# A long-convolution filter turned by VectorE in 32x32 blocks instead of by TensorE, and loaded in sixteen pieces

## The chip, the cores and the metric

The kernel runs on one core of one Trainium2 chip. The metric is device time in microseconds (us) of one execution, the median of several runs. A core has a matrix engine (TensorE, PE in the profile, with its weight loads as PEld), a vector engine (VectorE, DVE), a scalar engine (ScalarE, ACT), a general engine (GpSimd, POOL), a queue engine that here issues most transfers (SyncE, SP), and 16 DMA engines that carry out the transfers of all queues. Each engine works through its own list in order and waits on semaphores for the others.

## What is computed

The reference joins a long convolution with a gated feed-forward network. Cut to what matters:

```python
xn = _layernorm(A_q)                                   # 2048 x 512
k_shift = sum over t of k_pad[:, t:t+S, :] * shift_k   # four taps
kv = k_shift * v
y  = irfft(rfft(kv, 2S) * rfft(ssm_k, 2S))[:S] + kv * ssm_D
s  = xn * y
h  = gelu(xn @ w_gate) * (xn @ w_up)                   # 512 -> 1792
g  = silu(h @ w_down)                                  # 1792 -> 512
return A_q + s * g
```

The filter of the long convolution, `ssm_k`, is 512 channels by 2048 positions in bf16, 2 MB.

## The kernel before, in words

The tokens are cut into four quarters of 512. For each quarter, layer norm makes `XN`, a transpose makes `xnT`, 14 units of 128 hidden columns make the gate and up products (4 matmuls of 512 columns each), GELU and product fill `HT`, and the down products follow. The weights of gate and up come in four column parts (`FC`, line 793): part 0 serves units 0 and 1, part 1 units 2 to 5, part 2 ("third weights") units 6 to 9, part 3 units 10 to 13.

The convolution is a two-stage Fourier transform by matmuls. Stage 1 of the filter (`stage1("H", u)`, lines 956 to 991) multiplies the table `F1` with slice `u` of the turned filter `HTr`, for u from 0 to 7, in two products `i` of 512 columns, of two matmuls each; product `i` needs the row blocks 2i and 2i+1. The results go by ScalarE or VectorE to SBUF and then to a DRAM buffer `ZH`. The shift of k by four taps runs on VectorE (`kshift`, lines 1003 to 1029, 32 instructions of 2048 elements) and is multiplied with v; stage 1 of that product and stage 2 of both follow.

`ssm_k` lies in DRAM with channels as rows, and stage 1 needs positions on partitions. `load_h(k)` (line 820) loads 128 channels, rows of 4 KB, into `Hn[:, k, :]`. `h_transpose(k)` (lines 923 to 939) reads `Hn` as 32-bit words, two bf16 each, and turns it by eight TensorE transposes of 128x128 words (line 931, with an FP32 identity that line 696 makes on GpSimd), four into each of two PSUM banks; two instructions of VectorE or ScalarE (lines 638 and 641) bring them to `HTr`. Position 16a + 2t + (0 or 1) ends at partition a, slice t. `h_fold` (line 945, GpSimd) adds `ssm_D` to position 0 once all four row blocks are there; only the two products of slice 0 need it.

The order of work is written out. `ORDER` (line 26) is the order of the loads; all of them are issued by SP, and `SEQ` (line 27) lists all other tasks by number, from which each engine's list follows; a "b" marks the second choice of engine. `LAND` holds the planner's assumed landing times; they only serve its choice of buffers. Loads come first in SP's list, then the transposes by DMA, the ZK stores and so on. In TensorE's list before, the turning stands between the units: row blocks 0 and 1 after the gate product of unit 5, the rest up to the first products of units 6 to 9. GpSimd's list has the four copies of taps (line 1001) and the fold in between. The function `bass.AP` takes a list of [step, count], outermost first.

Of the kernel before, what the change touches and what calls it, by code (L numbers as in the profile page):

```python
# [16 lines left out]
NT = 16  # L17
# [8 lines left out]
ORDER = "x00 x01 x02 w0 w1 D0 h0 h1 h2 h3 s0 k0 w2 x1 k1 k2 w3 d0 d1 v0 v1 k3 v2 v3 x2 x3"  # L26
SEQ = (
# [25 lines left out]
LAND = {"x0_0": 2900, "h0": 11200, "x0_1": 3400, "x0_2": 4900, "D": 9850, "wg0": 5850, "wu0": 6800, "h1": 12500, "wg1": 8300, "wu1": 9800, "h2": 13850, "h3": 15500, "sk": 18000, "kh1": 19200, "kh113": 19400, "kz": 10800, "k0": 20600, "wg2": 22100, "wu2": 23600, "x1": 24900, "k1": 26200, "k2": 27500, "wg3": 29650, "wu3": 31200, "wd0": 33450, "wd1": 35700, "v0": 37050, "v1": 38400, "k3": 39750, "v2": 41100, "v3": 42450}  # L53
# [365 lines left out]
def build_kernel(nc, A_q, A_k, A_v, A_shift_k, A_ssm_k, A_ssm_D, B_w_gate, B_w_up, B_w_down, out):  # L419
    with ExitStack() as es0:  # L420
# [11 lines left out]
        def new(name, shape, dt):  # L432
            h = at(name, shape, dt, place["at"])
            place["at"] += size(shape, dt)
            return h
# [15 lines left out]
        ident32 = new("ident32", [128, 128], FP32)  # L451
# [91 lines left out]
        R_id, R_id32 = res("ident", ident[:]), res("ident32", ident32[:])  # L543
# [21 lines left out]
        R_Hn = [res(f"Hn{k}", Hn[:, k, :]) for k in range(KD)]  # L565
        R_HTr = [[res(f"HTr{t}_{k}", HTr[:, t, 256 * k:256 * k + 256]) for k in range(KD)] for t in range(NT // 2)]
# [96 lines left out]
        bHTr = [[B(f"HTr{k}_{h}") for h in range(2)] for k in range(KD)]  # L663
# [31 lines left out]
        def pool_id32():  # L695
            P(lambda h: h.tensor_scalar(ident32[:], K32[:], 0.0, None, ALU.is_equal), [R_id32], [R_K32])

# [15 lines left out]
        bcq, bck, bid32 = B("cq"), B("ck"), B("id32")  # L713
# [5 lines left out]
        S.add([("POOL", 560.0)], lambda e: pool_id32(), r=[bk32], w=[bid32])  # L719
# [72 lines left out]
        h_dr = A_ssm_k.rearrange("(kd p) n -> p kd n", p=128)  # L792
# [27 lines left out]
        def load_h(k, ring):  # L820
            load(f"h{k}", Hn[:, k, :], h_dr[:, k, :], [R_Hn[k]], [bHn[k]], 524288, ring)
# [99 lines left out]
        t_htr = [[] for _ in range(KD)]  # L921

        def h_transpose(k):
            pp = [B(f"psh{k}_{h}", pX) for h in range(2)]

            def tr(hf):
                def f(e):
                    for j in range(4):
                        o = bank(pp[hf])[:, 128 * j:128 * (j + 1)]
                        src = Hn[:, k, :].bitcast(FP32).rearrange("p (a t) -> p t a", t=NT // 2)[:, 4 * hf + j, :]  # L930
                        trk.op("PE", lambda h, o=o, src=src: h.transpose(o, src, ident32[:]), r=[R_Hn[k], R_id32], w=R_bank(pp[hf]), accum=True)  # L931
                return f
            for hf in range(2):
                h_tr_tasks.append(S.add([("PE", 4 * 110.0)], tr(hf), r=[bid32, bHn[k]], w=[pp[hf]], lat=150.0))
            for hf in range(2):
                def ev(e, h, hf=hf):
                    return copy(e, h, HTr[:, 4 * hf:4 * hf + 4, 256 * k:256 * (k + 1)], bank16(pp[hf]).rearrange("p (t x) -> p t x", x=256))
                t_htr[k].append(op([("ACT", act(1024)), ("DVE", dve(1024, 2))], ev, r=[pp[hf]], w=[bHTr[k][hf]],
                   rr=lambda hf=hf: R_bank(pp[hf]), ww=[x[k] for x in R_HTr[4 * hf:4 * hf + 4]]))

        for k in range(KD):
# [4 lines left out]
                    r=[bHD, *[bHTr[k][0] for k in range(KD)]], w=[bFold], rr=[R_D, *R_HTr[0]], ww=R_HTr[0])  # L946
# [9 lines left out]
        def stage1(x, u, Z):  # L956
# [11 lines left out]
            if x == "H":  # L968
                bl = B(f"low{u}")
                for i in range(2):  # L970
                    def pairs(e, i=i):
                        for b in range(2):
                            k = slice(64 * b, 64 * b + 64)
                            trk.op("PE", lambda h, b=b, k=k: h.matmul(ps(psl(pp[i]), b), lhsT=F1[k, :], rhs=HTr[k, u, 512 * i:512 * i + 512], start=True, stop=True, tile_position=(64 * b, 0)),  # L974
                                   r=[R_F1, *R_HTr[u][2 * i:2 * i + 2]], w=[R_ps[psl(pp[i])][b]], accum=True)
                    s1_tasks[x].append(S.add([("PE", T_FWD)], pairs, r=[bF1] + [bHTr[k][u // 4] for k in range(2 * i, 2 * i + 2)] + ([bFold] if u == 0 else []), w=[pp[i]], lat=150.0, mode=2))
# [403 lines left out]
```

## Time and profile before

| what | value |
|---|---|
| median of 3 runs | 188.6 us (188.5 to 189.69) |
| profiled execution | 188.14 us |
| its span, first to last instruction | 186.3 us |
| granted TensorE clock | 1.0 throughout |
| `Hn` loads in the profile | 4 of 512 KB, median 7.7 us from issue to landing |
| bytes read from HBM, written | 27.39 MB, 14.68 MB |

The page gives, for each engine, its busy time and share of the span; then a chain of work that ended last, followed back from the last instruction; then groups of instructions by line, with the number, the busy time in us, the mean of one in ns, and the idle time ahead of them with what ended it. In rows of the timeline and of the chain in order of time, the first number is the start in us, the second the length in us. In the view by stretches, "(x60)" is the number of instructions and "DMA share" the busy share of the 16 DMA engines.

### The profile page before, as it was taken

The numbers are of one execution on the slowest core, as the hardware profiler recorded it, in microseconds if no ns is written. First come the engines' busy times: TensorE is split into PE (matmuls) and PEld (weight loads), VectorE is DVE, ScalarE is ACT, GpSimd is POOL, SyncE is SP. The second block draws the span as 40 slices with busy tenths as digits, with TensorE's granted clock in tenths as the row PEclk, the third lists the DMA queues.
The fourth block names the chain that finished last, engine by engine and source line by source line (L and its number), as shares of the span: only waits on it lengthen the run. The fifth ranks groups of instructions, "written<-read, shape, count | busy, mean of one in ns | idle before, by whom it ended". The sixth has DMA issues, their size and how long they took to land.

```text
span 186.3 us, 3672 instructions
## 1 busy us (share of the span) xinstructions
PE 181.4 (97%) x1448; PEld 79.8 (43%) x1456; DVE 165.9 (89%) x250; ACT 137.9 (74%) x193; POOL 12.8 (7%) x27
## 2 busy tenths in 40 slices
PE   8899999999999999999999999999999999999993
PEld 2675544434343343344344334334343434445552
DVE  7868999999999999997499989999999987347995
ACT  4675897998589989995398977779797872236771
POOL 5503304000000000021000000000000000000000
PEclk9999999999999999999999999999999999999999
DMA  4999999999764799988999899694054344699155
GB/s 136 349 408 313 369 379 381 387 415 285 244 235 159 196 296 310 301 292 284 265 320 255 335 311 306 218 343 137 4 204 137 113 169 151 236 317 373 52 201 197
DMA packets 38646, 48.37 MB, mean 260 GB/s; under 512 B 9443, under 2 KB 28391, under 8 KB 38630
## 3 DMA queue, kind: packets, MB, share of 16 engines
q1 hardware_dynamic: 32102, 39.76, 65.4%
q10 hardware_dynamic: 6528, 8.39, 12.7%
q8 instruction: 11, 0.18, 0.4%
q14 instruction: 5, 0.04, 0.1%
HBM read 27.39 MB, written 14.68 MB: 226 GB/s over the span
## 4 chain that ended last, share of the span: by engine, by line
PE 89%; DVE 5%; ACT 4%; issue 1%; POOL 0%
PE psall L647 73%; PE psall L1043 6%; PE psall L1239 2%; PE psall L974 2%; PE psall L965 2%; PE psall L931 2%; ACT BO L638 2%; DVE G L1310 1%; ACT L1258 1%; DVE stats L860 1%; PE psall L1293 1%; DVE BO L641 1%; ACT G L1258 1%; PE psall L906 1%; DVE XN L882 0%
## 5 line engine op out<-in xcount | busy, mean ns | idle before, releaser
L647 PE MATMUL psall<-xnT,Wu 128*128 128x512 bf16 (+1 forms) x248 | 56.6, 359 | 0.0
L647 PE MATMUL psall<-xnT,Wg 128*128 128x512 bf16 (+1 forms) x248 | 55.9, 359 | 0.0
L1209 ACT ACTIVATE GE<-psall 128x512 bf16<-128x512 f32 x54 | 31.8, 604 | 10.5 <-PE psall L647 9.9
L647 PE MATMUL psall<-Wd,HT 128*128 128x512 bf16 (+1 forms) x174 | 38.3, 367 | 0.5 <-issue 0.2
L1218 DVE TENSOR_TENSOR HT<-psall,GE 128x512 bf16<-128x512 f32 x43 | 28.9, 685 | 5.0 <-PE psall L647 4.3
L647 PEld LDWEIGHTS psall<-xnT,Wg 128*128 128x128 bf16 x248 | 21.8, 98 | 26.6 <-issue 3.4
L647 PEld LDWEIGHTS psall<-xnT,Wu 128*128 128x128 bf16 x248 | 21.9, 98 | 26.3 <-issue 3.1
L647 PEld LDWEIGHTS psall<-Wd,HT 128*128 128x128 bf16 x182 | 16.6, 98 | 20.8 <-issue 2.6
L638 ACT ACTIVATE BO<-psall 128x1024 bf16<-128x1024 f32 x20 | 19.8, 1023 | 6.8 <-PE psall L1293 2.8
L1146 DVE TENSOR_TENSOR HSW<-KB,HSW 128x2048 bf16<-128x2048 bf16 x16 | 19.0, 1217 | 0.1
L638 ACT ACTIVATE KB<-psall 128x1024 bf16<-128x1024 f32 x14 | 13.7, 1024 | 2.1 <-PE psall L1043 2.1
L638 ACT ACTIVATE HSW<-psall 128x1024 bf16<-128x1024 f32 x14 | 13.8, 1026 | 1.9 <-PE psall L1043 1.9
L1026 DVE TENSOR_TENSOR KAC<-KAC,KTM 128x2048 bf16<-128x2048 bf16 x12 | 14.6, 1216 | 0.1
L1024 DVE TENSOR_TENSOR KTM<-KK,SKB 128x2048 bf16<-128x2048 bf16 x12 | 14.6, 1214 | 0.0
L1250 ACT ACTIVATE G<-psall 128x512 bf16<-128x512 f32 x12 | 7.1, 597 | 9.8 <-PE psall L647 9.8
L638 ACT ACTIVATE AST<-psall 128x1024 bf16<-128x1024 f32 x12 | 12.2, 1028 | 2.1 <-PE psall L965 2.0
L1239 PE MATMUL psall<-Wd,HT 128*64 128x512 bf16 (+1 forms) x112 | 12.2, 366 | 0.0
L1252 DVE SCALAR_TENSOR_TENSOR G<-G,psall 128x512 bf16<-128x512 bf16 x12 | 8.2, 679 | 4.0 <-ACT G L1250 4.0
L873 POOL TENSOR_TENSOR mv<-mv,NHALF 128x1 f32<-128x1 f32 (+1 forms) x7 | 6.5, 936 | 66.7 <-DVE mv L871 64.0
L860 DVE BATCH_NORM_STATS2 stats<-X 128x6 f32<-128x512 bf16 x16 | 10.1, 675 | 0.0
L638 ACT ACTIVATE XN<-psall 128x1024 bf16<-128x1024 f32 x9 | 9.1, 1023 | 1.3 <-PE psall L974 1.2
L1146 DVE TENSOR_TENSOR KB<-KB,HSW 128x2048 bf16<-128x2048 bf16 x8 | 9.5, 1214 | 0.0
(91 smaller groups left out, 176.8 us busy)
## 6 DMA issues: line engine op xcount, KB each, us to landing
BH<-ZH SPq DMA_DIRECT2D x8, 512.0 KB, 4.9
HSW<-HSW SPq DMA_DIRECT2D x16, 256.0 KB, 3.1
BK<-ZK SPq DMA_DIRECT2D x8, 512.0 KB, 5.4
ZI<-BO ACTq DMA_DIRECT2D x16, 256.0 KB, 2.4
BI<-ZI SPq DMA_DIRECT2D x8, 512.0 KB, 7.3
ZK<-AST SPq DMA_DIRECT2D x6, 512.0 KB, 3.8
ZH<-XN ACTq DMA_DIRECT2D x5, 512.0 KB, 4.4
Hn<-in_A_ssm_k_dram SPq DMA_DIRECT2D x4, 512.0 KB, 7.7
```

The lines of the kernel that those rows point to most:

```text
L638: return h.activation(o, i, ACTF.Copy, scale=scale)
L647: return h.matmul(o, lhsT=l, rhs=r, start=st, stop=sp)
L860: t_stats[t] = op([("DVE", 670.0)], lambda e, h, t=t: h.bn_stats(stats[:, t, :], X[:, t, :]), r=[bX[q][t % 4]], w=[bst[t]], rr=[R_X[t]], w ...
L1024: op([("DVE", dur)], lambda e, h, j=j, m=m: h.tensor_tensor(KTM[:, m.slot, :, :], kk(j), sk(j), ALU.mult), r=need + [bSKB[j], a], w=[m], r ...
L1026: op([("DVE", dur)], lambda e, h, m=m: h.tensor_tensor(KAC[:, a.slot, :, :], KAC[:, a.slot, :, :], KTM[:, m.slot, :, :], ALU.add), r=[m], ...
L1043: trk.op("PE", lambda h: h.matmul(ps(s, i)[b, :], lhsT=wt(col)[a, :], rhs=data(col)[a, :], start=n < 16, stop=n >= len(todo) - 16, tile_po ...
L1146: return hd.tensor_tensor(pair(KB, *(2 * DM * z for z in slots())) if to else x, k, x, ALU.mult)
L1209: op([("ACT", act(512))], lambda e, h: h.activation(GE[:, g.slot, :], bank(pg), ACTF.Gelu_apprx_tanh), r=[pg], w=[g], rr=lambda: R_bank(pg ...
L1218: op([("DVE", dve(512, 1))], lambda e, h: h.tensor_tensor(HT[:, q % 2, m, :], bank(pu), GE[:, g.slot, :], ALU.mult), r=[pu, g], w=[bHT[q][m]],
L1239: trk.op("PE", lambda h, m=m, i=i, c=c: h.matmul(pc()[c, :], lhsT=HT[:, q % 2, m, 128 * jt + 64 * i:128 * jt + 64 * i + 64], rhs=Wd[:, m, ...
L1250: op([("ACT", act(n))], lambda e, h, g=g, pc=pc: h.activation(g, pc(), ACTF.Tanh, scale=0.5), r=[p], w=[bt], rr=lambda p=p: R_bank(p), ww= ...
L1252: op([("DVE", dve(512, 1))], lambda e, h, g=g, pc=pc: h.scalar_tensor_tensor(out=g, in0=g, scalar=1.0, in1=pc(), op0=ALU.add, op1=ALU.mult ...
```

## The change

The filter is loaded in 16 pieces instead of four. Piece (k, c) takes channels 128k + 32c to 128k + 32c + 31; its source pattern runs over four column ranges of 512 positions, then over 32 channels, then over 512 elements (1 KB). So partition 32a + r holds channel 32c + r of the block, positions 512a to 512a + 511, in columns 512c to 512c + 511 of `Hn[:, k, :]`. One VectorE instruction for each k then turns all 32x32 blocks of words: it reads 1,024 words of each partition with a step of 8 words, and writes `HTr[:, :, 256k:256k+256]` for all eight slices. The 32 TensorE transposes, eight evictions, eight uses of PSUM banks and the FP32 identity go. All stage-1 products wait for whole row blocks, and the fold for all four.

```diff
-ORDER = "x00 x01 x02 w0 w1 D0 h0 h1 h2 h3 s0 k0 w2 x1 k1 k2 w3 d0 d1 v0 v1 k3 v2 v3 x2 x3"
+ORDER = "x00 x01 x02 w0 w1 D0 h0 h1 h2 h3 w2 x1 s0 k0 w3 k1 d0 k2 d1 v0 v1 k3 v2 v3 x2 x3"
...
-LAND = {"x0_0": 2900, "h0": 11200, ... }
+LAND = {"x0_0": 2950, ..., "h0_0": 10225, "h0_1": 10600, ..., "h3_3": 15850, "wg2": 17350, ... }
...
         def load_h(k, ring):
-            load(f"h{k}", Hn[:, k, :], h_dr[:, k, :], [R_Hn[k]], [bHn[k]], 524288, ring)
+            n = S_LEN // 4
+            for c in range(4):
+                src = bass.AP(A_ssm_k.tensor, A_ssm_k.offset + (128 * k + 32 * c) * S_LEN, [[n, 4], [S_LEN, 32], [1, n]])
+                load(f"h{k}_{c}", Hn[:, k, n * c:n * c + n], src, [R_Hnc[k][c]], [bHn[k]], 131072, ring)
...
         def h_transpose(k):
-            pp = [B(f"psh{k}_{h}", pX) for h in range(2)]
...
-                        trk.op("PE", lambda h, o=o, src=src: h.transpose(o, src, ident32[:]), r=[R_Hn[k], R_id32], w=R_bank(pp[hf]), accum=True)
...
-                t_htr[k].append(op([("ACT", act(1024)), ("DVE", dve(1024, 2))], ev, r=[pp[hf]], w=[bHTr[k][hf]],
-                   rr=lambda hf=hf: R_bank(pp[hf]), ww=[x[k] for x in R_HTr[4 * hf:4 * hf + 4]]))
+            def tr(e, h):
+                src = Hn[:, k, :].bitcast(I32).rearrange("p (c a t) -> p t c a", c=4, t=NT // 2)
+                return h.transpose(HTr[:, :, 256 * k:256 * (k + 1)].bitcast(I32), src)
+            h_tr_tasks.append(op([("DVE", dve(1024, 1))], tr, r=[bHn[k]], w=[bHTr[k]], rr=[R_Hn[k]], ww=[x[k] for x in R_HTr]))
...
-                    s1_tasks[x].append(S.add([("PE", T_FWD)], pairs, r=[bF1] + [bHTr[k][u // 4] for k in range(2 * i, 2 * i + 2)] + ([bFold] if u == 0 else []), w=[pp[i]], lat=150.0, mode=2))
+                    s1_tasks[x].append(S.add([("PE", T_FWD)], pairs, r=[bF1] + bHTr[2 * i:2 * i + 2] + ([bFold] if u == 0 else []), w=[pp[i]], lat=150.0, mode=2))
```

In `ORDER`, "w2" and "x1" (the third weights and the second quarter's tokens) now come right behind the filter, ahead of the taps "s0" with k's halo and of "k0"; "w3" comes ahead of "k1", and "d0", the first half of the down weights, ahead of "k2".

`SEQ` is new throughout, and its task numbers are shifted, since there are 12 more loads, 12 fewer turning tasks and one GpSimd task less. Read by engine, it says the following. TensorE starts as before up to the unit products of quarter 0; its first filter product is that of slice 6, row blocks 0 and 1, right after the gate product of unit 5. By then it has done 48 of the short matmuls (128 columns) and 12 of the long ones that it had done before its first turning in the kernel before, and 8 short and 8 long ones more. Then come 8 short matmuls, the gate and up products of unit 4 and the up product of unit 5 (12 long matmuls), and the products of slices 1 and 2 for row blocks 0 and 1; then the gate product of unit 7, the first work on the third weights; then the products for row blocks 2 and 3, between units 6 to 9. VectorE has its four turns among the first products of quarter 0, then the statistics of the second quarter (lines 860, 861, 872), three sums of stage 1 and the products of units 4 and 7, and then begins the shift of k. GpSimd's list has three copies of taps, the fold, and the fourth copy.

More of the change, by code (lines that the diff above doesn't have):

```diff
@@ L52 @@
 ISSUE = 470.0
[L53 removed]
+LAND = {"x0_0": 2950, "x0_1": 3400, "x0_2": 4900, "wg0": 5850, "wu0": 6800, "wg1": 8300, "wu1": 9800, "D": 9850, "kz": 10800, "h0_0": 10225, "h0_1": 10600, "h0_2": 10975, "h0_3": 11350, "h1_0": 11725, "h1_1": 12100, "h1_2": 12475, "h1_3": 12850, "h2_0": 13225, "h2_1": 13600, "h2_2": 13975, "h2_3": 14350, "h3_0": 14725, "h3_1": 15100, "h3_2": 15475, "h3_3": 15850, "wg2": 17350, "wu2": 18850, "x1": 20150, "sk": 22150, "kh1": 23850, "kh113": 24050, "k0": 25400, "wg3": 27000, "wu3": 28600, "k1": 29950, "wd0": 32650, "k2": 34000, "wd1": 36400, "v0": 37760, "v1": 39120, "k3": 40470, "v2": 41830, "v3": 43190}
 W_XT, W_SW, W_BK, W_BH, W_ZI, W_BI, W_ZK, W_MI, W_G1 = 850000, 690000, 685000, 688000, 310000, 575000, 600000, 329000, 150000
@@ L450, in build_kernel @@
         ident = new("ident", [128, 128], BF16)
-        ident32 = new("ident32", [128, 128], FP32)
         COLS = new("COLS", [128, 8], FP32)
@@ L542, in build_kernel @@
         R_MI = [res(f"MI{i}", MI[:, i, :, :]) for i in range(2)]
-        R_id, R_id32 = res("ident", ident[:]), res("ident32", ident32[:])
+        R_id = res("ident", ident[:])
         R_cols, R_col1 = (res(f"COLS{i}", COLS[:, i:i + 1]) for i in range(2))
@@ L565, in build_kernel @@
         R_Hn = [res(f"Hn{k}", Hn[:, k, :]) for k in range(KD)]
+        R_Hnc = [[res(f"Hn{k}_{c}", Hn[:, k, 512 * c:512 * c + 512]) for c in range(4)] for k in range(KD)]
         R_HTr = [[res(f"HTr{t}_{k}", HTr[:, t, 256 * k:256 * k + 256]) for k in range(KD)] for t in range(NT // 2)]
@@ L662, in build_kernel @@
         bHn = [B(f"Hn{k}") for k in range(KD)]
-        bHTr = [[B(f"HTr{k}_{h}") for h in range(2)] for k in range(KD)]
+        bHTr = [B(f"HTr{k}") for k in range(KD)]
         bHD = B("HD")
@@ L712, in build_kernel @@
         t_warm = S.add([("PE", N_WARM * 427.0)], warm_up, w=[warm])
-        bcq, bck, bid32 = B("cq"), B("ck"), B("id32")
+        bcq, bck = B("cq"), B("ck")
         S.add([("POOL", 420.0)], lambda e: pool_q(), w=[bcq])
@@ L718, in build_kernel @@
         S.add([("POOL", 700.0)], lambda e: pool_id(), r=[bk32], w=[bconst, bid])
-        S.add([("POOL", 560.0)], lambda e: pool_id32(), r=[bk32], w=[bid32])
         SIN_SCALE = 2.0 * math.pi / TURN * (1.0 - 2e-6)
@@ L920, in build_kernel @@
         h_tr_tasks = []
-        t_htr = [[] for _ in range(KD)]
         def h_transpose(k):
-            pp = [B(f"psh{k}_{h}", pX) for h in range(2)]
[L926 to L937, printed above, removed]
-                t_htr[k].append(op([("ACT", act(1024)), ("DVE", dve(1024, 2))], ev, r=[pp[hf]], w=[bHTr[k][hf]],
-                   rr=lambda hf=hf: R_bank(pp[hf]), ww=[x[k] for x in R_HTr[4 * hf:4 * hf + 4]]))
+            def tr(e, h):
+                src = Hn[:, k, :].bitcast(I32).rearrange("p (c a t) -> p t c a", c=4, t=NT // 2)
+                return h.transpose(HTr[:, :, 256 * k:256 * (k + 1)].bitcast(I32), src)
+            h_tr_tasks.append(op([("DVE", dve(1024, 1))], tr, r=[bHn[k]], w=[bHTr[k]], rr=[R_Hn[k]], ww=[x[k] for x in R_HTr]))
         for k in range(KD):
@@ L945, in build_kernel @@
         h_fold = op([("POOL", 1200.0)], lambda e, h: h.tensor_tensor(HT0, HT0, Drow[:], ALU.add),
-                    r=[bHD, *[bHTr[k][0] for k in range(KD)]], w=[bFold], rr=[R_D, *R_HTr[0]], ww=R_HTr[0])
+                    r=[bHD, *bHTr], w=[bFold], rr=[R_D, *R_HTr[0]], ww=R_HTr[0])
         t_ln = ln(0)
```

3 lines of the change are left out of this document (removed), and 44 rows, old and new, of the table SEQ.

## The prediction

> **What bounds the kernel now.** I read the page's head and its chain first, then the chain in order of time for the first 30 us, since everything that is changed lies there.
>
> ```profile
> span 186.3 us, 3672 instructions
> PE 181.4 (97%) x1448; PEld 79.8 (43%) x1456; DVE 165.9 (89%) x250; ACT 137.9 (74%) x193; POOL 12.8 (7%) x27
> PE 89%; DVE 5%; ACT 4%; issue 1%; POOL 0%
> ```
>
> TensorE is busy 181.4 of 186.3 us and is 89% of the chain of waits. It has 4.9 us of idle time in all, so work taken from it is worth almost its length, and time for which it has to wait is lost: there is no slack later to win it back. VectorE is next, with 20.4 us idle. The chain early on (start, length, what):
>
> ```profile
> 6.70 1.37 PE psall L647 x24
> 9.07 3.59 PE psall L647 x28
> 12.66 0.44 PE psall L931 x4
> 13.77 0.94 PE psall L931 x8
> 16.12 1.09 PE psall L931 x8
> 21.53 0.88 PE psall L931 x8
> 22.41 0.54 PE psall L974 x4
> 22.95 0.64 PE psall L931 x4
> 28.44 7.01 PE psall L647 x32
> ```
>
> L931 is the turning on TensorE. All 32 lie on the chain.
>
> **The change, part by part.** *Turning leaves TensorE.* 0.44 + 0.94 + 1.09 + 0.88 + 0.64 = 4.0 us off the chain. This is the whole possible gain: 188.1 to 184.1 us in the profiled execution (188.14, of which the span is 186.3; the median of the three runs, 188.6, stands 0.5 higher).
>
> *Turning comes to VectorE, evictions go.*
>
> ```profile
> L641 DVE COPY HTr<-psall 128x1024 bf16<-128x1024 bf16 x4 | 2.6, 682 | 0.6 <-PE psall L931 0.6
> L638 ACT ACTIVATE HTr<-psall 128x1024 bf16<-128x1024 bf16 x4 | 4.0, 1020 | 1.7 <-PE psall L931 1.7
> L641 DVE CAST XN<-psall 128x1024 bf16<-128x1024 f32 x1 | 1.2, 1214 | 0.0
> ```
>
> No row shows a block transpose on VectorE. One of them moves 1,024 words per partition, read with a step of 8 words. The lower bound is the 0.68 us of the 1,024-element copy, the upper one twice the 1.21 us of the 1,024-element cast, 2.4; I take 1.2, since that cast also goes one word at a time. Four cost 4.9 us against 2.7 for the evictions that go: 2.2 us more on VectorE, 4.1 less on ScalarE, in the kernel's first 26 us.
>
> *Loading: 16 pieces in place of 4 loads.* This decides.
>
> ```profile
> L620 SPq DMA_DIRECT2D Hn<-in_A_ssm_k_dram x4: 428/444/711, 4.7 to 6.1; - x4
> DMA to landing us min/median/max: 6.5/7.7/8.9
> ```
>
> ```profile
> core 0: us, PE busy (x) PEld busy (x) DVE busy (x) ACT busy (x) POOL busy (x), PEclk, DMA share, GB/s
> 10.00:15.50 5.50, 5.50 (x48) 3.83 (x46) 4.42 (x9) 3.44 (x9) 0.00 (x0) 1.00 1.03 406
> 15.50:25.00 9.50, 9.50 (x58) 5.21 (x57) 8.83 (x13) 7.39 (x10) 3.52 (x5) 1.00 1.05 344
> 31.00:45.00 14.00, 13.95 (x67) 5.88 (x67) 13.99 (x20) 12.84 (x20) 1.07 (x1) 1.00 1.08 377
> ```
>
> The four loads land at 4.7 + 6.5 = 11.2 to 6.1 + 8.9 = 15.0 us, 1.27 apart, so their data starts at 9.9. With 4 KB rows the 16 DMA engines are full (share 1.03) at 406 GB/s, 25.4 each; in the stretch with the weights' 1 KB rows at 344, 21.5 each. A new piece has 1 KB rows. Dealt over sixteen engines, the 2.1 MB take 6.1 us instead of 5.2: 0.9 later, which is hidden (below).
>
> But the source pattern of a piece is [4][32][512 elements]: four column ranges outermost, then 32 rows. Before, each large load has 64, 112 or 128 rows outermost on both sides. A queue that deals a transfer by its outermost entries can use no more engines than there are entries, four here. The table of DMA issues has three transfers with few rows, of 15, 1 and 3:
>
> ```profile
> KK<-in_A_k_dram SPq DMA_DIRECT2D x1, 45.0 KB, 11.3
> Drow<-in_A_ssm_D_dram SPq DMA_DIRECT2D x1, 1.0 KB
> KK<-AST SPq DMA_DIRECT2D x1, 3.0 KB
> ```
>
> The two smallest are the only issues of the kernel without a time to landing in that table, so their completion is reported in another way than that of a transfer on all engines. That fits a deal by outermost entries, though it shows nothing for a count of 4. The bounds are therefore 16 engines (no loss) and 4 (the loss below); the row nearest to 4 is the one of 3, and I take 4, the same four for every piece. The Trainium skill, page "DMA: Bandwidth & Descriptors", section "Why a DMA increments its semaphore by 16 and not by 1", speaks against the change outright: the number of engines is the largest up to 16 that divides the slowest dimension of both patterns, and on the SP and ACT queues it is the lowest-numbered ones. By that rule a piece has four, always the same; by the DMA share of this trace alone it could have sixteen; the sums are 203.8 and 185.5 us.
>
> On four engines at 21.5 GB/s the 2.1 MB take 24.4 us (at 25.4: 20.7). The sixteenth piece lands at 34.3, and the eighth, with which the first 256 channels are complete, at 9.9 + 12.2 = 22.1. Each later load also has a sixteenth of its bytes on each of these four and lands behind them: the third gate weights (512 KB, 1.5 us at 344 GB/s) at 35.8. The other twelve engines can run ahead, which helps no load to be complete.
>
> Now TensorE's own order. Up to its first filter product, the new order has what ended at 12.66 before, plus 8 short and 8 long matmuls (1.37 / 24 = 57 ns, 7.01 / 32 = 219 ns: 2.2 us): 14.9. That product needs the first two row blocks turned: 22.1 + 1.2 = 23.3. Behind it stand 8 short and 12 long matmuls and three filter products (0.27 each): 3.9 us. Then comes the first matmul on the third weights. Without a wait it would be reached at 18.8; the weights are there at 35.8. TensorE loses 17.0 us, in two gaps of about 8.4 and 8.6. Nothing can go ahead, since its queue is in order.
>
> *After the gap.*
>
> ```profile
> 0.76 4.42 PE L647 MATMUL psall<-const-bfloat16-1.0 128*128 128x512 bf16 x10 [0.76 <-PEq L1365]
> ```
>
> From idle, the first ten matmuls take 442 ns each, twice the 219 ns later. If a gap of 8 us brings this back, the next 4.4 us do 2.2 us of work. Behind the first gap it is hidden by the second; behind the second it costs 2.2. The bounds are 0 and 4.4. The Trainium skill, page "TensorE: Matmul & The Clock Gate", section "Why this matters for your kernels", asks for no gaps over some 3 us, because the clock falls to half; no gap of that length is in this trace, and by that rule the sum has the 2.2.
>
> *New order of the loads.* The third weights and x1 go ahead of the taps and of k0. On four engines k0 lands at 34.3 + 3.0 (weights) + 1.3 (x1) + 1.3 (taps) + 1.0 (halo) + 1.3 = 42.2, on sixteen at 23.9.
>
> ```profile
> 21.65 1.22 DVE L1020 TENSOR_TENSOR KAC<-KK,SKB 128x2048 bf16<-128x2048 bf16 x1
> L860 DVE BATCH_NORM_STATS2 stats<-X 128x6 f32<-128x512 bf16 x16 | 10.1, 675 | 0.0
> L1218 DVE TENSOR_TENSOR HT<-psall,GE 128x512 bf16<-128x512 f32 x43 | 28.9, 685 | 5.0 <-PE psall L647 4.3 <-ACT GE L1209 0.4
> ```
>
> VectorE starts its shift work at 21.65 now, so 20.5 later; about 5.5 us of other work (four statistics of 0.675 with their small followers, two products of 0.685, one 0.68 add) is moved ahead of it into the wait. That leaves 15.0 against TensorE's 17.0 − 4.0 + 2.2 = 15.2: the two fall behind together, and VectorE sets no later end. It is full from 31 to 45 (13.99 of 14.00), so it can't catch up; 2 us go into the upper end.
>
> *Queues.* SP issues 16 pieces of 0.44 us (7.0) in place of four (2.15), the third weights then at 11.7, long before their data: hidden by the backlog, otherwise 4.9 us. SP will also stall while four rings are full, as it does now:
>
> ```profile
> 11.09 4.48 SPq L620 DMA_DIRECT2D X<-in_A_q_dram  x1
> L945 POOL TENSOR_TENSOR HTr<-HTr,Drow 1x512 bf16<-1x512 bf16 x1 | 1.2, 1152 | 0.0
> L1001 POOL COPY SKB<-SKR 128x512 bf16<-128x512 bf16 x4 | 2.4, 648 | 8.4 <-DMA SKR<-in_A_shift_k_dram 8.4
> ```
>
> Behind it are only loads and, after the last, the transpose of the second quarter, which also waits for x1. On POOL the fold (1.15 us) still follows three tap copies (1.9) and now waits for the later taps (39.9 + 3.1 = 43 on four engines); the products that need it stand behind the quarter's last unit, near 50. Priced at nothing; without that cover it would be a wait of that length. The POOL instruction that made the FP32 identity goes; POOL is busy 7%. I price the rest of the new order at nothing, plus or minus 2 us.
>
> **The sum.** 188.1 − 4.0 + 17.0 + 2.2 = 203.3, and 0.5 for the median: 203.8 us. Lower end: 25.4 GB/s per engine (weights at 9.9 + 20.7 + 1.3 = 31.9, so 13.1 lost) and no slow restart: 188.1 − 4.0 + 13.1 + 0.5 = 197.7. Upper end: 4.4 for the restarts and 2 for VectorE: 208.
>
> **The rivals.** *Sixteen engines (faster).* If the pieces are dealt like any other load, the filter is there at 16.0, the third weights at 17.5, ahead of 18.8. TensorE gains its 4.0; VectorE has 2.2 more before the shift work and gets k0 2.3 later, so about 1 of the 4 is given back: 188.6 − 3.1 = 185.5. For it: DMA share 1.03 in all load stretches of this kernel. Against: no load of before has an outermost count between 3 and 15. It decides where the third weights land before 19 us.
>
> *Sixteen engines, VectorE eats the gain (no change).* Turns of 2.4 us each add 6.9 us net before the shift work, in a stretch where VectorE is full: TensorE's 4.0 are spent waiting for shifted blocks, 188 us. Against: 20.4 us of idle VectorE time in the whole.
>
> *Sixteen engines, and the order costs (slower).* The same with the 2 us of the new order or SP's 4.9 uncovered: 191 to 194.
>
> **How the numbers follow.** Four engines 0.68, as the nearest row (3 entries) is unlike that of a 128-row load, yet no row has 4; gain 0.19; no change 0.07; spread but slower 0.06. The prediction is that of the likeliest, 203.8, whose own range is 197.7 to 208. It holds some 0.58 within it, so the range goes down to the middle of the gain, 185: 0.58 + 0.10 + 0.07 + 0.06 = 0.81. Within 1% (186.7 to 190.5, about what a measurement of this kernel can tell from no change) are 0.07, faster 0.19, slower 0.74.
>
> **What would show it.** Right: the sixteen filter loads in the table of issues without a time to landing, or far beyond 15 us; DMA share near a quarter between 12 and 28 us; TensorE idle before L974 and again before the third weights; the shift work starting near 42. Wrong: DMA share still 1 there, the filter's turns on VectorE done by 17.5 and TensorE unbroken to 30 us. Turns of 2 us or more would show in VectorE's rows.

## The result and the profile after

The changed kernel takes 205.74 us in the median of 4 runs (205.57 to 206.38), the kernel before 188.77 us (188.5 to 189.69): a ratio of 1.0896, 95% interval 1.085 to 1.0941. It is slower by 17.0 us. All medians in this text are of executions in the faster of the chip's two states, which leaves out one of four of c_oldloads and one of ten of f_before_noturn. The profiled execution has a span of 203.8 us. First its page: busy time of all engines, TensorE's busy share in 40 slices of 5.1 us, the granted clock, the DMA share and the bytes moved.

```profile
PE 184.8 (91%) x1415; PEld 78.2 (38%) x1424; DVE 171.4 (84%) x249; ACT 134.8 (66%) x190; POOL 13.6 (7%) x26
...
PE   8892561999899999999999999999999999999992
...
PEclk9999588599999999999999999999999999999999
DMA  5822279999995937899699999549953413599436
GB/s 150 290 97 94 94 215 297 302 362 383 411 238 135 375 69 289 239 295 358 245 307 226 284 273 378 190 129 365 334 184 112 171 55 134 178 314 392 162 140 232
```

The damage is local. From the eighth slice on the PE row is 9 nearly throughout, as before. Slices 3 to 5 have a DMA share of 2 and 94 to 97 GB/s; in slices 4 to 7 TensorE is partly idle, and in slices 5 to 8 its clock is lower. The table of issues lists the sixteen filter loads without a time to landing, and the windows table over the same stretch shows the share to two digits (columns: TensorE, its weight loads, VectorE, ScalarE and GpSimd busy us, then clock, DMA share, GB/s):

```profile
Hn<-in_A_ssm_k_dram SPq DMA_DIRECT2D x16, 128.0 KB
```

```profile
10.00:15.00 5.00, 5.00 (x53) 3.39 (x51) 2.11 (x5) 2.52 (x7) 0.00 (x0) 1.00 0.28 98
15.00:20.00 5.00, 1.52 (x8) 0.49 (x5) 2.59 (x2) 0.58 (x2) 0.00 (x0) 1.00 0.27 94
20.00:25.00 5.00, 2.25 (x10) 0.99 (x11) 4.11 (x5) 1.10 (x2) 0.00 (x0) 0.51 0.27 94
25.00:30.00 5.00, 3.93 (x18) 1.43 (x16) 2.04 (x1) 3.04 (x4) 0.00 (x0) 0.81 0.71 194
30.00:35.00 5.00, 0.19 (x1) 0.14 (x2) 1.56 (x1) 0.02 (x1) 0.00 (x0) 0.88 1.05 304
```

A share of 0.27 to 0.28 where a full load stretch of this kernel shows 1.03 to 1.12 is a quarter: four engines of sixteen. This is also what the Trainium skill's rule, "DMA: Bandwidth & Descriptors", section "Why a DMA increments its semaphore by 16 and not by 1", gives for a slowest dimension of 4; here the trace agrees.

The trace shows the number of engines in two more ways, which the views above do not print. It keeps the events of each transfer's completion semaphore: 5 for each of the sixteen pieces, and 16 for each load of the filter in the kernel before. For the two smallest transfers, with one row and with three, it keeps 2 and 4, so the count stands one above the outermost entries, as for the pieces with their four. By its records of single packets, from 12 to 20 us never fewer than 4 and never more than 7 packets are under way at a time. The last events of the pieces come every 1.4 us from 10.9 to 26.2 us, those of the eighth at 20.7 and of the sixteenth at 33.4 us.

The timeline of the same stretch (start, duration, and in brackets the idle time before and what ended it) has both gaps, the four turns, and the events of the later steps:

```profile
15.11 2.02 DVE L923 STREAM_TRANSPOSE HTr<-Hn 128x1024 int32<-128x1024 int32 x1 [2.55 <-DMA Hn<-in_A_ssm_k_dram]
...
22.75 0.60 PE L959 MATMUL psall<-HTr,F 64*128 64x512 bf16 x2 [6.24 <-DVE HTr L923]
...
24.97 1.29 SPq L620 DMA_DIRECT2D Wg<-in_B_w_gate_dram  x1
...
33.44 2.01 DVE L923 STREAM_TRANSPOSE HTr<-Hn 128x1024 int32<-128x1024 int32 x1 [5.14 <-DMA Hn<-in_A_ssm_k_dram]
...
34.81 1.87 PE L647 MATMUL psall<-xnT,Wg 128*128 128x512 bf16 x4 [5.88 <-DMA Wg<-in_B_w_gate_dram]
...
43.27 1.15 POOL L930 TENSOR_TENSOR HTr<-HTr,Drow 1x512 bf16<-1x512 bf16 x1
...
44.96 1.65 DVE L1005 TENSOR_TENSOR KAC<-KK,SKB 128x2048 bf16<-128x2048 bf16 x1
```

TensorE waits 6.24 us for the first turned rows and 5.88 us for the third gate weights. The fourth turn starts at 33.44, so the last filter piece (33.4) and the third gate weights (34.7) arrive within about 2 us of each other. That detail decides one of the experiments.

### The profile page after: what moved, and what is told of

Same layout as the page of the kernel before. It is cut to its first block, busy times and chain, and to the rows that moved or that the text cites. A ratio compares the mean times of both kernels' runs of the same rounds, so it can differ in the third digit from the quotient of the medians.

```text
span 203.8 us, 3602 instructions
## 1 busy us (share of the span) xinstructions
PE 184.8 (91%) x1415; PEld 78.2 (38%) x1424; DVE 171.4 (84%) x249; ACT 134.8 (66%) x190; POOL 13.6 (7%) x26
## 3 DMA queue, kind: packets, MB, share of 16 engines
q10 hardware_dynamic: 6528, 8.39, 11.7%
## 4 chain that ended last, share of the span: by engine, by line
PE 67%; SPq 13%; DVE 11%; DMA 5%; issue 2%; ACT 1%; ACTq 0%; DVEq 0%
PE psall L647 56%; SPq L620 13%; DMA X<-in_A_q_dram 5%; PE psall L1028 5%; PE psall L950 2%; PE psall L1224 2%; DVE G L1307 2%; DVE G L1295 2%; DVE KAC L1005 1%; DVE stats L858 1%; PE psall L959 1%; DVE XN L965 1%; DVE G L1246 1%; DVE G L1245 1%; PE psall L1278 1%
## 5 line engine op out<-in xcount | busy, mean ns | idle before, releaser
L647 PE MATMUL psall<-xnT,Wg 128*128 128x512 bf16 (+1 forms) x248 | 58.8, 375 | 5.9 <-DMA Wg<-in_B_w_gate_dram 5.9
L647 PE MATMUL psall<-xnT,Wu 128*128 128x512 bf16 (+1 forms) x248 | 58.0, 369 | 0.7 <-DVE HT L1203 0.7
L647 PE MATMUL psall<-Wd,HT 128*128 128x512 bf16 (+1 forms) x173 | 38.3, 367 | 0.8 <-issue 0.5
L647 PEld LDWEIGHTS psall<-xnT,Wg 128*128 128x128 bf16 x248 | 22.8, 102 | 32.9 <-issue 10.1
L647 PEld LDWEIGHTS psall<-xnT,Wu 128*128 128x128 bf16 x248 | 22.5, 102 | 29.9 <-issue 5.4
L638 ACT ACTIVATE BO<-psall 128x1024 bf16<-128x1024 f32 x22 | 21.8, 1026 | 8.4 <-PE psall L1028 4.6
L923 DVE STREAM_TRANSPOSE HTr<-Hn 128x1024 int32<-128x1024 int32 x4 | 8.1, 2018 | 12.1 <-DMA Hn<-in_A_ssm_k_dram 12.1
L638 ACT ACTIVATE KB<-psall 128x1024 bf16<-128x1024 f32 x12 | 12.0, 1025 | 4.1 <-PE psall L1028 4.1
L959 PE MATMUL psall<-HTr,F 64*128 64x512 bf16 x32 | 7.0, 456 | 6.2 <-DVE HTr L923 6.2
L638 ACT ACTIVATE X<-psall 128x1024 bf16<-128x1024 f32 x6 | 6.3, 1053 | 8.7 <-PE psall L959 8.7
L638 ACT ACTIVATE XN<-psall 128x1024 bf16<-128x1024 f32 x10 | 10.2, 1031 | 1.7 <-PE psall L959 1.7
```

The costliest lines, as they stand in the source:

```text
L638: return h.activation(o, i, ACTF.Copy, scale=scale)
L647: return h.matmul(o, lhsT=l, rhs=r, start=st, stop=sp)
```

## The experiments

Each kernel was run beside the kernel before on the same chip (188.64 to 188.88 us). The theory was the prediction's: a quarter of the engines carries the filter, and all else follows. The rivals were that the number of pieces, the turn on VectorE or the new order cost the time, or that the slow issues on SP set the pace. The medians together; "after" and "before" in the third column name the kernel that was edited:

| kernel | us | from | edit | ratio to before, 95% interval |
|---|---|---|---|---|
| b_outer128 | 189.43 | before | 16 pieces of 1 KB rows, 128 outermost | 1.005 (1.0026 to 1.0073) |
| b_outer8 | 198.09 | before | 16 pieces, 8 outermost | 1.05 (1.0468 to 1.0531) |
| b_outer4 | 208.42 | before | 16 pieces, 4 outermost | 1.1041 (1.1001 to 1.1081) |
| a_rows_outer | 193.12 | after | 32 rows outermost, 32-partition targets | 1.0234 (1.0198 to 1.0271) |
| c_full128 | 190.34 | after | 128 rows outermost | 1.0088 (1.0059 to 1.0117) |
| c_src32 | 191.33 | after | 32 rows outermost, 128-partition targets | 1.0132 (1.0073 to 1.0191) |
| c_contig | 189.01 | c_full128 | turn reads words in order | 0.9985 (0.9956 to 1.0014) |
| c_oldloads | 192.81 | c_full128 | old order of loads | 1.0205 (1.0128 to 1.0281) |
| d_w2first | 208.23 | after | third weights ahead of the filter | 1.1006 (1.0951 to 1.106) |
| f_before_noturn | 189.14 | before | no turning at all | 1.0015 (0.9986 to 1.0043) |
| f_after_noturn | 188.9 | c_full128 | no turning at all | 1.0005 (0.9975 to 1.0035) |
| b_newloads | 193.81 | before | new order of loads | 1.0287 (1.023 to 1.0343) |

### The outermost count alone: b_outer4, b_outer8, b_outer128

These leave the kernel before as it is (TensorE turns, old order) but for the filter load, which becomes 16 pieces:

```diff
-load(f"h{k}", Hn[:, k, :], h_dr[:, k, :], ...)
+for c in range(4):
+    src = bass.AP(..., 128 * k * S_LEN + n * c, [[S_LEN, 4], [4 * S_LEN, 32], [1, n]])   # b_outer4
+    src = bass.AP(..., 128 * k * S_LEN + n * c, [[S_LEN, 8], [8 * S_LEN, 16], [1, n]])   # b_outer8
+    src = bass.AP(..., 128 * k * S_LEN + n * c, [[S_LEN, 128], [1, n]])                  # b_outer128
+    dma(ring, Hn[:, k, n * c:n * c + n], src, ...)
```

Expected of b_outer4:

> The kernel before with nothing changed but the filter's load: 16 pieces of 128 channels by 512 positions, source [4][32][512 elements]. To get this shape the channels are taken in steps of four, so the filter's channels are permuted in the result. Turn on TensorE, order as before. Theory: the eighth and sixteenth pieces land near 21 and 32 us, the third weights near 37 instead of 21.8; TensorE reaches its first work on them at 23.4 now, so it loses 13 to 14 us and about 2 to the half rate behind the gaps: 202 to 206 us. Rivals 'VectorE's turns' and 'new order': neither is in this kernel, so it should stay at 188 to 190.

Of b_outer8:

> As the one with four entries outermost, but the source is [8][16][512 elements] (channels in steps of eight, so permuted in the result). Theory: eight engines, DMA share near 0.5 from 10 to 21 us, a piece every 0.7 us, the last at 21, the third weights near 26, 2.5 to 4 us lost: 191 to 193 us. If the shape costs something else, such as a slow path for any source of three dimensions, it should come out like the one with four entries, 202 to 206.

Of b_outer128:

> The kernel before with the filter loaded in 16 pieces of 128 rows of 1 KB, source [128][512 elements], channels in their order. The rival that 1 KB rows and twelve more issues on SP are what costs, by itself: it would put this at 200 or more. Theory: all sixteen engines, about 0.9 us later for the filter and what follows it, 188 to 190 us.

Windows of 10 to 20 us, of b_outer4, then b_outer8, then b_outer128:

```profile
10.00:15.00 5.00, 2.87 (x16) 1.16 (x14) 2.65 (x5) 2.26 (x7) 0.00 (x0) 1.00 0.28 95
15.00:20.00 5.00, 2.27 (x16) 1.97 (x16) 1.12 (x2) 0.38 (x1) 0.00 (x0) 0.57 0.27 95
```

```profile
10.00:15.00 5.00, 4.15 (x32) 2.36 (x30) 3.33 (x7) 2.74 (x8) 0.00 (x0) 1.00 0.54 187
15.00:20.00 5.00, 2.54 (x18) 1.60 (x18) 2.13 (x5) 2.16 (x3) 0.00 (x0) 1.00 0.86 234
```

```profile
10.00:15.00 5.00, 5.00 (x48) 3.65 (x47) 2.73 (x7) 2.55 (x7) 0.00 (x0) 0.93 1.12 352
15.00:20.00 5.00, 5.00 (x45) 3.43 (x42) 4.38 (x9) 3.16 (x5) 0.08 (x1) 1.00 1.03 297
```

The share goes 0.28, 0.54, 1.12, and the bytes per second go with it: 95, 187, 352. The engines used are as many as the outermost entries, 4 and 8, and the time follows: 208.42, 198.09 and 189.43 us. The events of the pieces' semaphores say the same, 5, 9 and 16 for each piece, and so do the packets under way from 12 to 15 us: 4 to 7, 8 to 13 and 16 to 23. This also speaks against SP as the cause. Its issues of a piece are slow with 4 outermost (1.31 us, median), but where the issues set the pace, as in c_src32 below, the packets under way from 12 to 15 us swing from 1 to 20; here they stay at 4 and a few more. The number and row size of the pieces cost at most 0.7%. For 4 the mechanism and the size were near (2 us above the expected range); for 8 the mechanism held and the size was 5 us too low. Its share climbs to 0.86 while the filter is still loading: later loads need the same eight engines too, which the estimate had left out. The pieces land every 0.7 us up to 17.6 us, but every 1.0 to 1.3 us behind that, so the last lands at 24.5 instead of 21 and the third gate weights at 30.9 instead of 26.

### The changed kernel on all engines: a_rows_outer, c_full128, c_src32

Three ways to put many entries outermost in the changed kernel:

```diff
-src = [[n, 4], [S_LEN, 32], [1, n]]            target Hn[:, k, n*c:n*c+n]       # after
+src = [[S_LEN, 32], [32*S_LEN, 4], [1, n]]     target Hn[32*c:32*c+32, k, :]    # a_rows_outer
+src = [[S_LEN, 128], [1, n]]                   target Hn[:, k, n*c:n*c+n]       # c_full128
+src = [[S_LEN, 32], [32*S_LEN, 4], [1, n]]     target Hn[:, k, n*c:n*c+n]       # c_src32
```

> The changed kernel with its sixteen pieces cut the other way: a piece is one column range for all 128 channels of a block, its source [32 channels][4 channel groups][512 elements], its target 32 partitions. Same bytes, same 1 KB rows, same number of transfers, same turn and order; only the outermost count of the source is 32 instead of 4. Theory (a transfer uses no more DMA engines than it has outermost entries): the filter is there by 16 to 20 us, the DMA share is back near 1 from 10 us on, the gaps before the first filter product and before the third weights go, 184.5 to 188 us. Rival 'small rows and many issues': nothing changes, 204 to 207. Rival 'VectorE's turns of 2 us': nothing changes either, since they stay. Rival 'new order of loads': nothing changes.

It took 193.12, some 5 us above what the theory gave. So four engines were the larger part of the loss, if not all of it. Two differences from the kernel before were left in its trace: DMA moved only 238 GB/s in the filter's stretch, and the turns took 2.0 us each. c_full128 removes the first:

> The changed kernel with only the source pattern of the filter's pieces changed: [S_LEN, 128] rows outermost, the target over all 128 partitions (channels and positions come out mixed, so the output is not the reference's; bytes, rows and number of pieces are the same). It differs from a_rows_outer (193.1) only in that each piece goes to 128 partitions and not to 32. Theory A, the slower loads into 32 partitions (238 to 253 GB/s) are the larger part of what a_rows_outer has above before: the last piece lands near 17.5 instead of 20.5, the half-rate matmuls go, and the time is 189.5 to 191. Theory B, VectorE's turns of 2.0 us are (8.0 us in front of the shift work, against 2.6 us of copies and a cast of 1.2 in the kernel before): 192 to 194.

190.34 us: theory A, the loads into 32 partitions. c_src32 then parts target and source:

> The changed kernel with the source pattern of a_rows_outer (32 rows outermost, four stretches of 1 KB of each) and the target over all 128 partitions of c_full128 (channels and positions come out mixed, so the output is not the reference's). It parts the two things in which a_rows_outer (193.1) and c_full128 (190.3) differ. If the 32-partition target is the price, the loads run near 350 GB/s and the time is 189.7 to 191; if the source pattern is, 238 to 253 GB/s and 192.5 to 194.

Windows of 2 us, a_rows_outer, c_full128, c_src32:

```profile
9.00:11.00 2.00, 2.00 (x25) 1.42 (x23) 1.58 (x5) 1.87 (x5) 0.00 (x0) 1.00 1.15 229
...
13.00:15.00 2.00, 1.99 (x13) 0.79 (x10) 2.00 (x2) 0.60 (x1) 0.00 (x0) 1.00 1.14 238
```

```profile
9.00:11.00 2.00, 2.00 (x26) 1.43 (x24) 1.43 (x4) 1.99 (x5) 0.00 (x0) 1.00 1.10 347
...
13.00:15.00 2.00, 2.00 (x13) 0.80 (x10) 2.00 (x3) 0.98 (x2) 0.00 (x0) 1.00 1.10 351
```

```profile
9.00:11.00 2.00, 2.00 (x26) 1.43 (x24) 1.42 (x4) 1.97 (x5) 0.00 (x0) 1.00 1.11 349
...
13.00:15.00 2.00, 2.00 (x13) 0.91 (x11) 2.00 (x3) 0.98 (x2) 0.00 (x0) 1.00 0.63 197
```

At 9 to 11 us, a_rows_outer and c_src32 load the filter with the same source pattern; 349 GB/s into 128 partitions stand against 229 into 32, both at a full share. So the target is the price, and a share over 1 doesn't mean that bytes move at full rate. But c_src32 doesn't hold 349: its share drops to 0.63. The rows of the filter's issues on SP (min/median/max ns, first and last start) say why, c_src32 first, then c_full128:

```profile
L620 SPq DMA_DIRECT2D Hn<-in_A_ssm_k_dram x16: 593/603/1174, 4.7 to 15.0; - x16
```

```profile
L620 SPq DMA_DIRECT2D Hn<-in_A_ssm_k_dram x16: 427/432/707, 4.7 to 12.2; - x16
```

SP needs 603 ns per piece instead of 432, which is 217 GB/s for pieces of 128 KB; its last issue is at 15.0, and from 13 us on the engines wait for issues. The source pattern alone is not what makes an issue slow: in a_rows_outer, with the same source, a piece takes 432 ns too. That c_src32 ended a little above the 191 of either expectation fits this; its interval overlaps that of c_full128, so the difference between those two is not settled.

### The turn itself: c_contig

```diff
-src = Hn[:, k, :].bitcast(I32).rearrange("p (c a t) -> p t c a", c=4, t=NT // 2)
+src = Hn[:, k, :].bitcast(I32).rearrange("p (t c a) -> p t c a", c=4, t=NT // 2)
```

> c_full128, and the turn reads its words in order instead of every eighth word (positions are mixed once more, so the output is not the reference's). If the step of 32 bytes in the turn's read is what makes it 2.02 us, the turn takes near 1.2 us, 4 x 0.8 = 3.2 us of VectorE go, and the time falls by 1.5 to 3.2 us under c_full128. If 2.02 us is the price of 1024 words of 4 bytes in 32x32 blocks however they are read, the turn stays at 2.0 us and the time within 0.7 us of c_full128.

The groups of VectorE in c_full128 (from 5 to 50 us) and in c_contig:

```profile
L923 DVE STREAM_TRANSPOSE HTr<-Hn 128x1024 int32<-128x1024 int32 x4 | 8.0, 2020 | 0.1
```

```profile
L923 DVE STREAM_TRANSPOSE HTr<-Hn 128x1024 int32<-128x1024 int32 x4 | 4.8, 1230 | 0.9 <-DMA Hn<-in_A_ssm_k_dram 0.9
```

Reading every eighth 4-byte word (a step of 32 bytes) costs 0.79 us of 2.02. The 1.2 us of the prediction would have been right for a turn without that step. The time falls by 1.3 us, slightly under the expected 1.5: of 3.2 us less on VectorE, about 40% reached the end. This isn't a version to use, since the layout needs that step.

### The two waits have one cause: d_w2first

```diff
-ORDER = "x00 x01 x02 w0 w1 D0 h0 h1 h2 h3 w2 x1 s0 k0 ..."
+ORDER = "x00 x01 x02 w0 w1 D0 w2 h0 h1 h2 h3 x1 s0 k0 ..."
```

> The changed kernel (filter on four engines) with one move: the third weights are issued ahead of the filter's pieces and not behind them. The theory of the prediction, two waits of TensorE with a cause each: third weights land near 12, the wait for them (5.9 us at 28.9 to 34.8, and the half-rate matmuls behind it) goes, the wait for the turned filter stays and comes some 1 to 3 us later since the pieces begin later; the time is 205.7 - 6 - 1 + 2 = 197 to 201. Rival, the filter alone sets the end (its pieces land at the same pace whatever else waits, and all of TensorE's later work on the spectrum hangs on the last of them): the wait that goes comes back elsewhere, 204 to 207.

208.23 us: the rival. TensorE in its timeline:

```profile
26.05 0.61 PE L959 MATMUL psall<-HTr,F 64*128 64x512 bf16 x2 [11.02 <-DVE HTr L923]
...
40.46 0.61 PE L959 MATMUL psall<-HTr,F 64*128 64x512 bf16 x2 [7.46 <-DVE HTr L923]
```

With the third weights there early, the wait for them is gone and both waits are for the turned filter, 18.5 us in all against 12.1. The products on row blocks 2 and 3 stand close behind the third weights in TensorE's list, and in the changed kernel the fourth turn (ending at 35.45) was hidden under the wait for those weights and the four matmuls behind it. The third gate weights now land at 11.8 us, but the last filter piece at 38.3 instead of 33.4. Putting loads ahead of the transfer that four engines carry only delayed that transfer here.

### What the turning was worth: f_before_noturn, f_after_noturn

Both load the filter straight into `HTr` and leave the turning out, the first in the kernel before, the second in c_full128:

```diff
-load(f"h{k}", Hn[:, k, :], h_dr[:, k, :], [R_Hn[k]], ...)
+load(f"h{k}", HTr[:, 2*k:2*k+2, :], h_dr[:, k, :], R_HTr[2*k] + R_HTr[2*k+1], ...)    # f_before_noturn
-trk.op("PE", lambda h: h.transpose(...))      -op([("ACT", ...), ("DVE", ...)], ev, ...)
...
+load(f"h{k}_{c}", HTr[:, 2*k + c//2, n*(c%2):n*(c%2)+n], src, ...)                   # f_after_noturn
-return h.transpose(HTr[:, :, 256*k:256*(k+1)].bitcast(I32), src)
```

> The kernel before with the turning left out: the filter is loaded straight to where the turned filter lies, and neither TensorE's 32 transposes nor the eight copies out of PSUM are made (so the output is not the reference's). It is the most that any cheaper turning can bring under the old order. The prediction's term, 4.0 us of TensorE on the path that sets the end: 184.3 to 185.3. Rival, what TensorE really spends is the difference of its busy time between the kernel before and c_contig (181.4 - 179.9 = 1.5 us) and the rest of the 4.0 lies in pipelined overlap: 186.8 to 187.8. Second rival, the old order has another limit right behind: 188 to 189.

> c_full128 with the turning left out: pieces of 128 rows of 1 KB go straight to where the turned filter lies and VectorE does no turn (so the output is not the reference's); the new order of loads and work stays. It differs from c_full128 (190.3) by 4 x 2.02 us of VectorE. If the turn's time on VectorE is what keeps the new order from gaining, 184.5 to 187. If the new order itself costs what TensorE saves, 188 to 190.

Neither is faster than the kernel before: 1.0015 (0.9986 to 1.0043) and 1.0005 (0.9975 to 1.0035). TensorE in f_before_noturn, and then the same place in the kernel before:

```profile
20.12 0.61 PE L973 MATMUL psall<-HTr,F 64*128 64x512 bf16 x4
24.38 4.45 PE L647 MATMUL psall<-xnT,Wg 128*128 128x512 bf16 x12 [3.65 <-DMA Wg<-in_B_w_gate_dram]
```

```profile
21.36 1.05 PE L931 MATMUL psall<-ident,Hn 128*128 128x128 f32 x8
22.34 0.61 PE L974 MATMUL psall<-HTr,F 64*128 64x512 bf16 x4
22.88 0.71 PE L931 MATMUL psall<-ident,Hn 128*128 128x128 f32 x4
23.43 2.75 PE L647 MATMUL psall<-xnT,Wg 128*128 128x512 bf16 x12
```

Without the turning TensorE comes to the third weights sooner, at 20.7 us, and waits 3.65 us for them; the twelve matmuls behind the wait then take 4.45 us in place of 2.75. (This execution took 190.8 us, one of the longest of its kernel; most of the others show a full clock and so no such slow matmuls.) Only a part of the wait is the turning's doing. In the kernel before the third gate weights land at 21.8 us, in time for the 23.4 at which they are needed; without the turning they would be waited for from 20.7 on, 1.1 us by this estimate. In f_before_noturn they land only at 24.3, since its last filter load lands at 18.6 instead of 15.1; why loading straight into `HTr` is later stays open. So the turning had filled some time in which the weights were still on their way, but that all of its 4 us were off the path that sets the end is not shown. In the new order there is no wait for the weights, and yet nothing is won: the second expectation's last case. TensorE reaches its first block of down products no sooner (f_after_noturn with its two larger waits, then the kernel before):

```profile
16.16 0.39 PE L959 MATMUL psall<-HTr,F 64*128 64x512 bf16 x2 [1.25 <-DMA HTr<-in_A_ssm_k_dram]
...
36.41 1.90 PE L647 MATMUL psall<-xnT,Wu 128*128 128x512 bf16 x8 [0.89 <-DVE HT L1203]
...
39.00 6.64 PE L647 MATMUL psall<-Wd,HT 128*128 128x512 bf16 x30 [0.16 <-issue]
```

```profile
38.53 0.81 PE L647 MATMUL psall<-Wd,HT 128*128 128x512 bf16 x3
```

Waits of 2.1 us have come in place of the turning. The first, 1.25 us, belongs to this run alone: it puts the fourth row block's pieces where slice 6 lies, so the first filter product waits for the thirteenth piece (landed at 16.0) and not for the eighth (13.7). Neither run is therefore the clean limit of a turn that costs nothing, and why the new order gains nothing stays open.

### The order of the loads: c_oldloads, b_newloads

```diff
-ORDER = "... h0 h1 h2 h3 w2 x1 s0 k0 w3 k1 d0 k2 d1 v0 ..."     # new
+ORDER = "... h0 h1 h2 h3 s0 k0 w2 x1 k1 k2 w3 d0 d1 v0 ..."     # old; c_oldloads in c_full128, b_newloads the other way in before
```

> c_full128 with the order of the loads as before (taps s0 and k0 ahead of the third weights, then x1, k1, k2, w3, d0, d1); every other order stays new. Theory C, the new order of loads costs part of what is left: k0 lands some 3 us sooner, VectorE's shift work starts sooner, and the time falls by 1 to 3 us under c_full128. Theory B, VectorE is full from 15 us on and takes the taps when it is through with its turns: within 1 us of c_full128, or up to 2 us above it, since the third weights land some 3 us later.

> The kernel before with one part of the change alone: the new order of the loads (third weights and x1 right behind the filter, taps and k0 behind them; w3, k1, d0, k2, d1). TensorE's and VectorE's order and the turning stay. If the new order is a help by itself, the time is 187 to 188.5. If it only fits the new order of work: VectorE's shift work, which starts at 21.65 and has no idle time behind it, waits 2 to 3 us for k0 and the time is 190 to 193.

Both lose: c_oldloads is 2.5 us over c_full128, past the 2 us that theory B allowed; b_newloads is 4.9 us over before, 0.8 past its second case. One row of each, TensorE in c_oldloads and VectorE in b_newloads (of executions of 194.1 and 195.5 us, above the medians):

```profile
25.20 1.70 PE L647 MATMUL psall<-xnT,Wg 128*128 128x512 bf16 x4 [3.77 <-DMA Wg<-in_B_w_gate_dram]
```

```profile
26.08 1.93 DVE L1020 TENSOR_TENSOR KAC<-KK,SKB 128x2048 bf16<-128x2048 bf16 x1 [4.36 <-DMA KK<-in_A_k_dram]
```

Each order of the loads fits its own order of work: with TensorE free of the turning, the third weights are needed first; with VectorE free of it, the taps and k0 are. Given the new order of work, the new order of loads was a needed part of the change and not what costs. The new order of work was not tested alone; c_full128 keeps it, so it has no part in the 15.4 us below, but it may have one in what c_full128 still lacks.

## Why the prediction was right

The mechanism was right: four engines, the filter late, TensorE idle in two gaps, a half-rate restart. That four engines cost the time was tested with a single edit: c_full128 differs from the changed kernel in the source pattern alone and takes 190.34 us, 15.4 of the 17.0 us less. The number, 203.8 against 205.74 us, is nearer than its terms: they missed in both directions.

How the terms came out, in busy and idle time of TensorE. The pages of the kernel before and of the changed kernel lack 8 and 9 matmul records, all of one group of down products (174 and 173 of 182). The page of c_src32 lacks the same 9, its clock is full from 6 us on, and its matmuls are those of the changed kernel, so the three can be compared. Its row:

```profile
PE 179.1 (95%) x1415; PEld 75.9 (40%) x1424; DVE 170.0 (90%) x249; ACT 134.5 (71%) x190; POOL 12.4 (7%) x26
```

- **Turning gone, −4.0.** 181.4 − 179.1 = 2.3 us of busy time less. As time nothing of it was seen: f_before_noturn gains nothing in the old order and f_after_noturn nothing in the new, though each has a wait of its own. In the changed kernel this didn't matter much, since TensorE waits for data anyway.
- **Two gaps, 17.0.** Idle time is 203.8 − 184.8 = 19.0 us, against 186.3 − 181.4 = 4.9 before: 14.1 more. The two gaps are 6.2 and 5.9 instead of 8.4 and 8.6, 12.1 in all. The first is shorter mainly because TensorE came to it at 16.5 and not at 14.9: the short matmuls ahead ran at half rate up to 9.7 us in this execution (eight in 0.83 us, in c_full128 in 0.45). The second is shorter because the work between the gaps ran at half rate (6.2 us instead of 3.9) and because the weights landed at 34.7, not 35.8. The first matmul on the third weights starts at 34.8, 16.0 after the 18.8 of the prediction.
- **Restart, 2.2.** Busy time is 184.8 − 179.1 = 5.7 us above that of c_src32 for the same matmuls. By the timelines of the changed kernel and c_full128, some 1.5 us of this lie ahead of the first gap, 1.9 between the gaps and 2.5 behind the second. The prediction counted only the last, and that was about right: there four matmuls of 512 columns take 1.87 us where the rows at full rate have 1.03. The clock of 0.51 and 0.81 in the windows from 20 to 30 us is the restart behind the first gap. The Trainium skill, "TensorE: Matmul & The Clock Gate", section "Why this matters for your kernels", asks for no idle gaps over some 3 us, since the clock falls back to half behind them; the trace agrees, as gaps of 6 us here bring the half rate. In a_rows_outer a gap of 2.47 us, ending at 17.45, was followed by the half rate too (clock 0.73 and 0.50 in the two us from 18 on), so 3 us is no safe bound here.
- The sum of these is 14.1 + 5.7 − 2.3 = 17.5 us, the difference of the two spans, where the prediction had 17.0 + 2.2 − 4.0 = 15.2. So the number came near partly by luck: a smaller wait, against a larger loss of clock, a smaller saving and 2.0 us of idle time outside the two gaps.
- **The turn, 1.2 us.** Mis-sized: 2.02 us, inside the bounds of 0.68 to 2.4. The step of 32 bytes is the cause (c_contig). While the filter is late the fourth turn is hidden under the wait for the weights; once it isn't, the step costs about 1.3 us (c_contig).
- **SP.** Sixteen issues of 0.44 us and the third weights at 11.7: wrong. SP was held about 1.3 us per piece, and the third weights were issued at 24.97. The row of the issues in the changed kernel:

```profile
L620 SPq DMA_DIRECT2D Hn<-in_A_ssm_k_dram x16: 552/1307/1657, 4.7 to 23.6; - x16
```

  It most likely cost nothing here, as a part of their data needs the four engines anyway: the weights landed 1.3 us behind the last piece. No run has fast issues and four engines, so this is argued and not shown. That later loads stand wholly behind the filter was not quite right: from the weights' issue on, the last three pieces land every 1.8 to 2.0 us instead of every 1.4, so the four engines carry both side by side.
- **Late taps.** The fold at 43.27 (43 predicted) and the shift work at 44.96 (42.2). The taps landed at 40.5 (39.9) and k0 at 43.1 (42.2), and GpSimd began the taps' copies as soon as they were there. VectorE came to the shift 1.9 us behind k0, as it was still at the work placed ahead of it, the second quarter's statistics among it, whose tokens landed only at 38.2.
- **The rivals.** The forecast of 185.5 us for sixteen engines would have been wrong by 5: c_full128 has them and takes 190.34. The step that fails there is "TensorE gains its 4.0". The case called "VectorE eats the gain" (188) was nearer, though for another reason: even with no turn on VectorE the time is 188.9 (with that run's own wait of 1.25 us).

No version here beats the kernel before. The nearest version of the changed kernel that keeps the filter's layout is a_rows_outer, 2.3% slower (interval 2.0 to 2.7). What a turn that cost nothing would bring is not settled, since both runs without a turn brought waits of their own; in these two orders of work nothing points to a gain.

## What to carry to other kernels

When a load is cut into pieces, look at the outermost count of both patterns of each piece: a count of 4 put a 2 MB load on four engines, and the loads behind it were late as well. Before you price the work that a change takes off the busiest engine, ask which data that engine would need next and whether they are there; leaving the work out in a run of its own helps to answer it, provided that the loads land in that run when they did before (in f_before_noturn they did not). Fewer rows outermost is not the only trap: aim each piece at all 128 partitions, and look at bytes per second beside the DMA share.

## What the runs showed of the hardware

- A piece whose target is 32 partitions moved 229 to 239 GB/s at a DMA share of 1.14 to 1.15; the same source pattern into 128 partitions moved 349 at 1.11.
- A piece with 4 or 8 outermost entries shows 5 or 9 events of its completion semaphore in the trace, one with 128 shows 16; the DMA share was 0.27 to 0.28, 0.54 and 1.10 to 1.12.
- The time of an issue on SP depends on the patterns: 0.43 us for a piece of 128 rows, 0.43 for 32 rows by four stretches into 32 partitions, 0.60 for the same source into 128 partitions, 1.31 while only four engines drain it.
- A turn of 128x1024 words of 4 bytes in 32x32 blocks takes 1.23 us on VectorE read in order, and 2.02 us read with a step of 32 bytes.
